# Attention and an ELU layer on one core: all of batch 0's q, k and v are issued ahead of the weights, and pairs 2 and 3 move into steps 0 to 3

## Chip, cores and metric

One core of one Trainium2 chip runs the kernel. The metric is device time in microseconds (us) of one execution, as the median of several runs. Differences within 0.3% count as no change here.

## What is computed

A sliding-window attention feeds a two-layer network with an ELU between the layers:

```python
# q, k, v: (8, 8, 576, 64) float32: batch, heads, positions, head size
scores = (q @ k.T) / sqrt(64)
scores = where(|pos_i - pos_j| <= 32, scores, -1e9)
attn = softmax(scores)               # over the keys
x = (attn @ v)                       # -> (8*576, 8*64) = (4608, 512)
h = x @ w_in                         # w_in (512, 2048)
g = where(h > 0, h, exp(min(h, 0)) - 1)
out = g @ w_out                      # w_out (2048, 512), out (4608, 512) float32
```

## The kernel before

The order of instructions on each engine is the order in which the program text issues them; nothing reorders them afterwards.

**Attention.** A batch has 9 blocks of 64 queries. Two blocks are a *pair*, and there are 36 pairs over the 8 batches; pairs 0 to 3 need batch 0 alone. `cast_qk` turns loaded float32 q and k (tile `f`, one for q and one for k) into bf16 (`qkb`), `transpose_qk` transposes these on TensorE into PSUM (`ptx`) and copies them to `qT` and `kT`. For a pair `scores` multiplies kT and qT into `psS` and takes the exponential into `pu` on ScalarE, `mask` multiplies by 0 or 1 into `pm` on VectorE, `pv` multiplies by v, `normalize` divides by the row sums into `x_st`, `x_transpose` transposes and `x_evac` copies the result into `xT`. Odd blocks read v shifted by 64 positions: `Vo` is a second copy of `Ve`, made by two DMAs on SP's queue in `rotate_v` (L122), each of which waits until the v loads that it reads have landed.

**Layer.** `xT[t]` holds 256 tokens (two pairs). The work on it is cut into 8 units of 256 hidden columns each, and the 18 tiles of 256 tokens give 144 steps. Step kk runs `mm1(kk)` (8 matmuls into `ps`, L435, then `e_sb` on ScalarE and `m_sb` on VectorE), and `mm2(kk - 2)` (4 matmuls into `psY`, L462); `elu` makes `g_sb` at the start of the step after. Steps 0 to 3 work on xT[0] (pairs 0 and 1), steps 4 to 7 on xT[1] (pairs 2 and 3), then the two alternate until step 15. Between these, attention tasks are put into named places of a step ("first", "dve", "mid", "end") by `at(step, place, ...)`, and they run in the loop

```python
run(kk, "first");  elu(kk - 1);  run(kk, "dve");  mm1(kk)
run(kk, "mid");    mm2(kk - 2);  run(kk, "end")
```

**Loads.** Queue q1 of the profile (hardware_dynamic) takes what SP issues: q and k, the `Vo` rotations, the outputs. Queue q0 (software_dynamic) takes what POOL issues: v and the weights, which are cast on the way. For batches 0 and 1, q and k come in halves of 288 positions, HALF_A and HALF_B. `gate(src)` (L130) is a DMA of one element on SP's queue that reads a piece of a weight tile; SP waits there until that weight's load has landed, and so holds back all that is behind it. w_in and w_out come in four chunks each; steps 0 and 1 need the first of w_in, steps 2 and 3 the second.

Of the kernel before, what the change touches and what calls it, by code (L numbers as in the profile page):

```python
# [15 lines left out]
def _bap(ap, new_ap, off=0):  # L16
    return bass.AP(tensor=ap.tensor, offset=ap.offset + off,
                   ap=[list(x) for x in new_ap])
# [3 lines left out]
def kernel(  # L22
# [15 lines left out]
    D_MODEL = H * D  # L38
# [8 lines left out]
    VS = 5  # L47
# [6 lines left out]
    NFO = D_FF // 128  # L54
# [39 lines left out]
    w_out_sb = wpool.tile([128, NFO, D_MODEL], BF16, name="w_out_sb")  # L94
# [4 lines left out]
    WHOLE, HALF_A, HALF_B = (0, SJ), (0, SJ // 2), (1, SJ // 2)  # L99
    qk_f = {}  # L100

    def load_qk(b, which, part):
        z, nj = part
        if (b, which) not in qk_f:
            qk_f[b, which] = lpool.tile([SP_, H * SJ * D], FP32,
                                        tag=f"f{which}", name=f"f{which}")
        t = qk_f[b, which]
        n = H * nj * D
        nc.sync.dma_start(
            out=t[:, z * n:(z + 1) * n].rearrange("p (h x) -> p h x", h=H),  # L110
            in_=(q, k)[which][b, :, z * SP_ * nj:(z + 1) * SP_ * nj, :]
            .rearrange("h (p j) d -> p h (j d)", j=nj))

    def load_v(b, m):
        lo = 128 * m - WIN
        p0 = max(0, -lo)
        p1 = min(128, S - lo)
        nc.gpsimd.dma_start(  # L118
            out=V_e[b % 3][p0:p1, m, :, 0:D],
            in_=v[b, :, lo + p0:lo + p1, :].rearrange("h p d -> p h d"))  # L120

    def rotate_v(b, m0=0, m1=VS - 1):  # L122
        e, o = V_e[b % 3], V_o[b % 3]
        nc.sync.dma_start(out=o[0:64, m0:m1], in_=e[64:128, m0:m1])
        nc.sync.dma_start(out=o[64:128, m0:m1], in_=e[0:64, m0 + 1:m1 + 1])
# [4 lines left out]
    def gate(src):  # L130
        n = gates[0]
        gates[0] += 1
        nc.sync.dma_start(out=gate_t[:, n:n + 1], in_=src)

    def load_w_in(c):
        w = D_FF // 4
        nc.gpsimd.dma_start(
            out=w_in_sb[:, :, c * w:(c + 1) * w],
            in_=moe_w_in[:, c * w:(c + 1) * w].rearrange(
                "(o p) f -> p o f", p=128))  # L140

    def load_w_out(c):
        n = NFO // 4
        nc.gpsimd.dma_start(
            out=w_out_sb[:, c * n:(c + 1) * n, :],
            in_=moe_w_out[c * n * 128:(c + 1) * n * 128, :].rearrange(
                "(o p) f -> p o f", p=128))

    def w_in_at(c):
        return w_in_sb[0:1, 0, (c + 1) * (D_FF // 4) - 1:(c + 1) * (D_FF // 4)]  # L150
# [9 lines left out]
    ident = cpool.tile([128, 128], BF16)  # L160
    make_identity(nc, ident)

    for which in range(2):
        load_qk(0, which, HALF_A)
    for m in (1, 2, 0):
        load_v(0, m)
    rotate_v(0, 0, 2)
    load_w_in(0)


# [16 lines left out]
        channel_multiplier=-1)  # L187
    kinds = ["FE", "EE", "EL", "LF"]

    for which in range(2):  # L190
        load_qk(0, which, HALF_B)
    for m in (3, 4):
        load_v(0, m)
    rotate_v(0, 2, VS - 1)
    load_w_out(0)
    load_w_in(1)
    load_w_out(1)
# [1 line left out]
    def kind(jb):  # L199
        qb = jb % NQB  # L200
        return "F" if qb == 0 else "L" if qb == NQB - 1 else "E"
# [10 lines left out]
    def cast_qk(b, which, part, hps, eng):  # L212
        z, nj = part
        hp0, nh = hps[0], 2 * len(hps)
        n = H * nj * D
        s_ = qk_f[b, which][:, z * n + 2 * hp0 * nj * D:
                            z * n + (2 * hp0 + nh) * nj * D]
        s_ = _bap(s_, [s_.ap[0], [nj * D, nh], [D, nj], [1, D]])
        t = lpool.tile([SP_, nj, nh * D], BF16, tag=f"b{which}", name="qkb",
                       bufs=4)  # L220
        qk_b[b, which, z, hp0] = t
        copy_on(eng, _bap(t, [t.ap[0], [D, nh], [nh * D, nj], [1, D]]), s_)

    def transpose_qk(b, which, part, hps, evac, tag="t0"):
        z, nj = part
        src = qk_b.pop((b, which, z, hps[0]))
        nh = len(hps)
        W = 512 if nh > 1 else 1024
        pt = ps_tile([128, nh, W], BF16, tag, "ptx")
        for g in range(nh):  # L230
            for j in range(nj):
                nc.tensor.transpose(  # L232
                    pt[:, g, j * SP_:(j + 1) * SP_],
                    src[:, j, g * 128:(g + 1) * 128], ident[0:SP_, 0:SP_])
        n = SP_ * nj
        if which == 0:
            T, c0 = qT[b % 2], z * n
        else:
            T, c0 = kT[b % 2], WIN + z * n
        d = T[:, hps[0]:hps[0] + nh, c0:c0 + n]  # L240
        pitch = d.ap[1][0] if nh > 1 else n
        copy_on(evac,
                _bap(d, [d.ap[0], [pitch, nh], [nj, SP_], [1, nj]]),
                _bap(pt, [pt.ap[0], [W, nh], [1, SP_], [SP_, nj]]))
# [3 lines left out]
    def scores(i, tag="s"):  # L248
        psS = ps_tile([128, 2, 512], FP32, tag, "psS")
        for z in range(2):  # L250
            jb = 2 * i + z
            b, qb = jb // NQB, jb % NQB
            for h in range(H):
                hp, base = h // 2, 64 * (h % 2)
                nc.tensor.matmul(  # L255
                    psS[:, h % 2, hp * 128 + z * QB:hp * 128 + (z + 1) * QB],
                    lhsT=kT[b % 2][base:base + 64, hp, QB * qb:QB * qb + 128],
                    rhs=qT[b % 2][base:base + 64, hp, QB * qb:QB * (qb + 1)],
                    start=True, stop=True)
        pu = apool.tile([128, H, 2 * QB], BF16, tag="pu")  # L260
        nc.scalar.activation(  # L261
            pu, _bap(psS, [psS.ap[0], [1, 1024]]), AX.Exp, scale=SCALE)
        st[i] = [psS, pu, None, None, tag]

    def mask(i):
        psS, pu, _, _, _ = st[i]
        pm = apool.tile([128, H, 2 * QB], BF16, tag="pm")
        m0 = kinds.index(kind(2 * i) + kind(2 * i + 1))
        mm = masks[:, m0:m0 + 2, :]
        nc.vector.tensor_mul(  # L270
            pm, pu, _bap(mm, [mm.ap[0], [0, H], [1, 2 * QB]]))
        st[i][2] = pm
# [50 lines left out]
    def front_qk(part, tags):  # L323
        for g in range(2):
            hps = (2 * g, 2 * g + 1)
            cast_qk(0, 0, part, hps, nc.vector)
            cast_qk(0, 1, part, hps, nc.scalar)
            transpose_qk(0, 0, part, hps, nc.scalar, tags[g])
            transpose_qk(0, 1, part, hps, nc.vector, tags[2 + g])

    front_qk(HALF_A, ("h0", "h1", "y0", "y1"))
    for i, tag in ((0, "s"), (1, "u")):
        scores(i, tag)
    for fn in (mask, pv, normalize, x_transpose, x_evac):
        for i in (0, 1):
            fn(i)

    gate(w_in_at(0))
    for which in range(2):
        load_qk(1, which, HALF_A)  # L340
    for m in range(3):
# [21 lines left out]
    def at(kk, slot, fn, *args):  # L363
        tasks.setdefault((kk, slot), []).append((fn, args))
# [11 lines left out]
        at(kk + 3, "dve", x_evac, i)  # L376


    at(1, "mid", front_qk, HALF_B, ("y0", "y1", "y0", "y1"))
    for i, tag in ((2, "s"), (3, "u")):  # L380
        at(1, "mid", scores, i, tag)
        at(2, "first", mask, i)
    for i in (2, 3):
        at(2, "first", pv, i)
        at(3, "dve", normalize, i)
        at(3, "mid", x_transpose, i)
        at(4, "dve", x_evac, i)
    at(4, "dve", swap_pools)

    allh = tuple(range(HP))  # L390
# [12 lines left out]
    for b in range(2, B):  # L403
        k0 = HALF * (first_pair(b) - 2)
        for n in range(2 * HP):
            if b == 2:
                which, hp, kk, ahead = n // HP, n % HP, 20 + n, 2
            else:
                which, hp, kk, ahead = n % 2, n // 2, k0 - 15 + 2 * n, 5
# [106 lines left out]
```

## Time and profile before

| | us |
|---|---|
| median of 3 runs (359.62 to 360.46) | 359.78 |
| the profiled execution's own time | 362.43 |
| its span, first to last instruction | 360.7 |
| TensorE (PE) busy | 319.6 |
| VectorE (DVE) busy | 254.3 |
| ScalarE (ACT) busy | 167.4 |

The profile is of one execution, which took 2.65 us more than the median of the runs. PE is busy for 89% of the span; in 40 slices of 9 us its busy share is below 8 tenths only in the first five (0, 3, 6, 2 and 7 tenths), the ninth (7) and the last (4). The granted TensorE clock is 0.969 of full speed over the span; it is about half in the fourth and fifth slices.

### The profile page before, as it was taken

What the parts mean: (1) busy time and instruction counts of PE and PEld (TensorE: products, weight loads), DVE (VectorE), ACT (ScalarE), POOL (GpSimd) and SP (SyncE); (2) the same over time, 40 slices, a digit from 0 to 9 for tenths busy, and PEclk for the clock granted to TensorE, in tenths of its full rate; (3) what the DMA queues carried; (4) which work ended last, traced back from release to release, by engine and by line L of the source; (5) the groups of instructions that cost most, each with busy time, mean ns of one, the idle gap of its engine ahead of it and who ended that gap; (6) DMA issues with size and microseconds to landing.
All of it is one profiled execution on the core that took longest, in us unless ns stands there. A gap on an engine that the chain in (4) does not pass through costs nothing.

```text
span 360.7 us, 8157 instructions
## 1 busy us (share of the span) xinstructions
PE 319.6 (89%) x3356; PEld 214.9 (60%) x3408; DVE 254.3 (71%) x474; ACT 167.4 (46%) x262; POOL 85.0 (24%) x108
## 2 busy tenths in 40 slices
PE   0362789979899999999999999999999999999994
PEld 0241556645666666666666666666666666666662
DVE  4442456858677877887877777878877777777763
ACT  2413227355565555355555544455545454434341
POOL 8711300452184400412520331421100000000000
PEclk9995599989999999999999999999999999999999
DMA  9999999779949966930778693963011210101011
GB/s 164 202 237 212 219 150 221 165 49 260 198 134 215 162 42 121 205 81 2 138 47 196 129 154 19 204 131 117 15 47 44 78 58 2 60 2 59 2 58 58
DMA packets 63944, 42.00 MB, mean 116 GB/s; under 512 B 38564, under 2 KB 58020, under 8 KB 63908
## 3 DMA queue, kind: packets, MB, share of 16 engines
q1 hardware_dynamic: 22180, 32.58, 37.8%
q0 software_dynamic: 41728, 8.92, 32.0%
q8 instruction: 26, 0.43, 0.5%
q14 instruction: 10, 0.08, 0.1%
HBM read 36.70 MB, written 9.44 MB: 128 GB/s over the span
## 4 chain that ended last, share of the span: by engine, by line
PE 73%; DVE 11%; DMA 7%; ACT 4%; issue 3%; SPq 0%; DVEq 0%
PE ps L435 33%; PE psY L462 29%; DMA f<-in_k_dram 7%; PE ptx L232 4%; DVE g_sb L448 3%; PE psS L255 3%; PE psS L282 3%; ACT e_sb L441 3%; PE psXT L303 2%; DVE m_sb L443 2%; DVE x_st L294 2%; DVE y_sb L471 1%; ACT qkb L208 1%; DVE pm L270 1%; DVE kT L210 1%
## 5 line engine op out<-in xcount | busy, mean ns | idle before, releaser
L441 ACT ACTIVATE e_sb<-ps 128x512 f32<-128x512 f32 x144 | 86.0, 597 | 167.6 <-PE ps L435 167.6
L435 PE MATMUL ps<-xT,w_in_sb 128*128 128x256 bf16 x1152 | 153.1, 277 | 5.6 <-DVE xT L313 4.7
L462 PE MATMUL psY<-w_out_sb,g_sb 128*128 128x512 bf16 x524 | 142.5, 382 | 3.2 <-issue 0.4
L435 PEld LDWEIGHTS <-w_in_sb 128*128 128x128 bf16 x1152 | 110.4, 99 | 37.8 <-issue 7.5
L443 DVE TENSOR_SCALAR m_sb<-e_sb 128x512 bf16<-128x512 f32 x144 | 71.0, 493 | 63.8 <-ACT e_sb L441 63.4
L448 DVE SCALAR_TENSOR_TENSOR g_sb<-ps,m_sb 128x512 bf16<-128x512 f32 x144 | 99.4, 690 | 13.6 <-PE psS L282 0.5
L462 PEld LDWEIGHTS <-g_sb 128*128 128x128 bf16 x576 | 51.1, 98 | 38.8 <-issue 1.1
L210 POOL CAST qkb<-f 96x768 bf16<-96x768 f32 x48 | 42.1, 900 | 120.5 <-PE ptx L232 51.8
L118 POOL DMA_DIRECT2D Ve<-in_v_dram x40 | 34.3, 862 | 51.6 <-PE psS L282 33.6
L232 PE MATMUL ptx<-ident,qkb 96*128 96x96 bf16 x384 | 28.2, 216 | 18.7 <-DVE qkb L210 11.0
L261 ACT ACTIVATE pu<-psS 128x1024 bf16<-128x1024 f32 x36 | 36.4, 1018 | 3.4 <-PE psS L255 3.3
L232 PEld LDWEIGHTS <-qkb 96*128 96x128 bf16 x384 | 23.9, 103 | 21.4 <-DVE qkb L210 11.7
L270 DVE TENSOR_TENSOR pm<-pu,masks 128x1024 bf16<-128x1024 bf16 x36 | 26.1, 726 | 3.8 <-ACT pu L261 3.6
L294 DVE TENSOR_TENSOR x_st<-psS,rc 128x512 bf16<-128x512 f32 x36 | 24.9, 692 | 1.2
L282 PEld LDWEIGHTS <-pm 128*64 128x64 bf16 x576 | 12.9, 115 | 18.9 <-DVE pm L270 9.1
L208 ACT COPY qT<-ptx 128x576 bf16<-128x576 bf16 (+1 forms) x30 | 20.0, 666 | 4.4 <-PE ptx L232 4.4
L282 PE MATMUL psS<-Ve,pm 128*64 128x65 bf16 x320 | 16.9, 202 | 3.2 <-DVE pm L270 3.2
L303 PEld LDWEIGHTS <-x_st 128*128 128x128 bf16 x144 | 9.6, 100 | 14.9 <-DVE x_st L294 12.9
L208 ACT COPY kT<-ptx 128x576 bf16<-128x576 bf16 (+1 forms) x26 | 17.4, 670 | 0.0
L255 PE MATMUL psS<-qT,kT 64*128 64x64 bf16 x576 | 15.5, 196 | 1.6 <-DVE kT L210 1.3
L303 PE MATMUL psXT<-ident,x_st 128*128 128x128 bf16 x144 | 14.6, 225 | 2.5 <-DVE x_st L294 2.1
L255 PEld LDWEIGHTS <-kT 64*128 64x128 bf16 x576 | 11.2, 98 | 8.9 <-issue 7.0
(29 smaller groups left out, 88.5 us busy)
## 6 DMA issues: line engine op xcount, KB each, us to landing
out_dram<-y_sb SPq DMA_DIRECT2D x18, 512.0 KB, 3.0
f<-in_q_dram SPq DMA_DIRECT2D x6, 1152.0 KB, 11.5
f<-in_k_dram SPq DMA_DIRECT2D x6, 1152.0 KB, 15.3
Vo<-Ve SPq DMA_DIRECT2D x12, 260.0 KB, 4.3
Ve<-in_v_dram POOLq DMA_DIRECT2D x24, 128.0 KB, 8.1
f<-in_q_dram SPq DMA_DIRECT2D x4, 576.0 KB, 12.3
f<-in_k_dram SPq DMA_DIRECT2D x4, 576.0 KB, 13.6
w_in_sb<-in_moe_w_in_dram POOLq DMA_DIRECT2D x4, 512.0 KB, 18.4
```

The source lines that it names most:

```text
L118: nc.gpsimd.dma_start(out=V_e[b % 3][p0:p1, m, :, 0:D], in_=v[b, :, lo + p0:lo + p1, :].rearrange("h p d -> p h d"))
L208: nc.scalar.copy(d_, s_)
L210: eng.tensor_copy(d_, s_)
L232: nc.tensor.transpose(pt[:, g, j * SP_:(j + 1) * SP_], src[:, j, g * 128:(g + 1) * 128], ident[0:SP_, 0:SP_])
L255: nc.tensor.matmul(psS[:, h % 2, hp * 128 + z * QB:hp * 128 + (z + 1) * QB], lhsT=kT[b % 2][base:base + 64, hp, QB * qb:QB * qb + 128], rh ...
L261: nc.scalar.activation(pu, _bap(psS, [psS.ap[0], [1, 1024]]), AX.Exp, scale=SCALE)
L282: nc.tensor.matmul(psS[QB * z:QB * (z + 1), par, hp * VD:(hp + 1) * VD], lhsT=pm[:, par * HP + hp, z * QB:(z + 1) * QB], rhs=vv[:, qb // 2 ...
L435: nc.tensor.matmul(ps[:, j, :], lhsT=w_in_sb[:, do, fo * 128:(fo + 1) * 128], rhs=xT[t][:, do, :], start=(do == 0), stop=(do == NDO - 1))
L441: nc.scalar.activation(e_sb, ps, AX.Exp)
L443: nc.vector.tensor_scalar(m_sb, e_sb, -1.0, None, ALU.add)
L448: nc.vector.scalar_tensor_tensor(g_sb, psH.pop(kk), 0.0, m_t.pop(kk), ALU.max, ALU.min)
L462: nc.tensor.matmul(psY[t][ts], lhsT=g_sb[:, j, ts * 128:(ts + 1) * 128], rhs=w_out_sb[:, s * FG + j, :], start=(s == 0 and j == 0), stop=( ...
```

## The change

The second half of batch 0's q and k is issued on SP's queue right behind the first, ahead of the first rotation, and all five v loads of batch 0 ahead of the first weight chunk on POOL's queue. Casting and transposing that half (`front_qk(HALF_B, ...)`) moves from the middle of step 1 to a place between the masks and the value products of pairs 0 and 1, with other PSUM tags. The tasks of pairs 2 and 3 start in step 0 where they started in step 1. The first gate now reads the last element that chunk 0 of w_out brings, where it read w_in's chunk 0. No instruction is added or removed.

```diff
--- before.py
+++ after.py
@@ -160,11 +160,13 @@
     ident = cpool.tile([128, 128], BF16)
     make_identity(nc, ident)
 
-    for which in range(2):
-        load_qk(0, which, HALF_A)
-    for m in (1, 2, 0):
+    for part in (HALF_A, HALF_B):
+        for which in range(2):
+            load_qk(0, which, part)
+    for m in (1, 2, 0, 3, 4):
         load_v(0, m)
     rotate_v(0, 0, 2)
+    rotate_v(0, 2, VS - 1)
     load_w_in(0)
 
 
@@ -187,11 +189,6 @@
         channel_multiplier=-1)
     kinds = ["FE", "EE", "EL", "LF"]
 
-    for which in range(2):
-        load_qk(0, which, HALF_B)
-    for m in (3, 4):
-        load_v(0, m)
-    rotate_v(0, 2, VS - 1)
     load_w_out(0)
     load_w_in(1)
     load_w_out(1)
@@ -331,11 +328,14 @@
     front_qk(HALF_A, ("h0", "h1", "y0", "y1"))
     for i, tag in ((0, "s"), (1, "u")):
         scores(i, tag)
-    for fn in (mask, pv, normalize, x_transpose, x_evac):
+    for i in (0, 1):
+        mask(i)
+    front_qk(HALF_B, ("h0", "h1", "y0", "y1"))
+    for fn in (pv, normalize, x_transpose, x_evac):
         for i in (0, 1):
             fn(i)
 
-    gate(w_in_at(0))
+    gate(w_out_sb[0:1, NFO // 4 - 1, D_MODEL - 1:D_MODEL])
     for which in range(2):
         load_qk(1, which, HALF_A)
     for m in range(3):
@@ -376,15 +376,13 @@
         at(kk + 3, "dve", x_evac, i)
 
 
-    at(1, "mid", front_qk, HALF_B, ("y0", "y1", "y0", "y1"))
     for i, tag in ((2, "s"), (3, "u")):
-        at(1, "mid", scores, i, tag)
-        at(2, "first", mask, i)
-    for i in (2, 3):
-        at(2, "first", pv, i)
-        at(3, "dve", normalize, i)
-        at(3, "mid", x_transpose, i)
-        at(4, "dve", x_evac, i)
+        at(0, "mid", scores, i, tag)
+        at(1, "dve", mask, i)
+        at(1, "mid", pv, i)
+        at(2, "dve", normalize, i)
+        at(2, "mid", x_transpose, i)
+        at(3, "dve", x_evac, i)
     at(4, "dve", swap_pools)
 
     allh = tuple(range(HP))
```

SP's queue, from the start of the program: before, where f_115 and f_117 are q and k of batch 0, and f_280 q of batch 1:

```order
L109 DMA f_115<-in_q_dram 96x8x192
L109 DMA f_117<-in_k_dram 96x8x192
L124 DMA Vo_91<-Ve_88 64x1040
L125 DMA Vo_91<-Ve_88 64x1040
L109 DMA f_115<-in_q_dram 96x8x192
L109 DMA f_117<-in_k_dram 96x8x192
L124 DMA Vo_91<-Ve_88 64x1040
L125 DMA Vo_91<-Ve_88 64x1040
L133 DMA gate_t<-w_in_sb 1x1
L109 DMA f_280<-in_q_dram 96x8x192
```

and now, where f_320 is q of batch 1:

```order
L109 DMA f_115<-in_q_dram 96x8x192
L109 DMA f_117<-in_k_dram 96x8x192
L109 DMA f_115<-in_q_dram 96x8x192
L109 DMA f_117<-in_k_dram 96x8x192
L124 DMA Vo_91<-Ve_88 64x1040
L125 DMA Vo_91<-Ve_88 64x1040
L124 DMA Vo_91<-Ve_88 64x1040
L125 DMA Vo_91<-Ve_88 64x1040
L133 DMA gate_t<-w_out_sb 1x1
L109 DMA f_320<-in_q_dram 96x8x192
```

Both loads of the second half have moved ahead of the four rotation DMAs, and the gate reads w_out.

VectorE, from the evacuation of xT of pairs 0 and 1 to the masks of pairs 2 and 3, before:

```order
L313 COPY xT<-psXT 128x4x128 x2
L443 TENSOR_SCALAR m_sb<-e_sb 128x512
L448 SCALAR_TENSOR_TENSOR g_sb<-ps,m_sb 128x512
L443 TENSOR_SCALAR m_sb<-e_sb 128x512
L210 CAST qkb<-f_115 96x4x3x64
L210 COPY kT_86<-ptx 128x2x288
L210 CAST qkb<-f_115 96x4x3x64
L210 COPY kT_86<-ptx 128x2x288
L270 TENSOR_TENSOR pm<-pu,masks 128x1024 x2
```

and now, from behind the masks of pairs 0 and 1 to the masks of pairs 2 and 3:

```order
L207 CAST qkb<-f_115 96x4x3x64
L207 COPY kT_86<-ptx 128x2x288
L207 CAST qkb<-f_115 96x4x3x64
L207 COPY kT_86<-ptx 128x2x288
L288 RECIPROCAL rc<-psS 128x8
L291 TENSOR_TENSOR x_st<-psS,rc 128x512
L288 RECIPROCAL rc<-psS 128x8
L291 TENSOR_TENSOR x_st<-psS,rc 128x512
L310 COPY xT<-psXT 128x4x128 x2
L441 TENSOR_SCALAR m_sb<-e_sb 128x512
L446 SCALAR_TENSOR_TENSOR g_sb<-ps,m_sb 128x512
L267 TENSOR_TENSOR pm<-pu,masks 128x1024 x2
```

The two casts and two copies of the second half have moved from behind steps 0 and 1's `m_sb` to ahead of the first reciprocal, and the masks of pairs 2 and 3 follow the first `g_sb`.

## Rows read from the trace of the kernel before

**Rows 1.** The chain that ended last, in time order: start us, length us, what.

```profile
13.10 16.71 DMA f<-in_k_dram
...
39.34 0.65 PE psS L282 x16
...
43.52 1.69 PE ps L435 x8
...
47.80 1.03 PE ps L435 x8
...
49.70 0.87 PE ps L435 x8
...
75.37 1.53 PE ps L435 x8
...
79.43 0.89 PE ps L435 x8
```

**Rows 2.** Busy time by stretch (us): each engine, granted clock, DMA share, GB/s.

```profile
28.00:45.00 17.00, 9.18 (x101) 6.41 (x103) 6.31 (x12) 5.27 (x7) 4.44 (x6) 0.50 1.34 216
45.00:72.00 27.00, 25.04 (x244) 16.82 (x246) 18.56 (x34) 12.55 (x18) 4.77 (x6) 1.00 1.55 180
...
76.00:79.00 3.00, 3.00 (x21) 1.94 (x19) 0.43 (x1) 1.70 (x3) 1.01 (x2) 0.50 0.13 5
```

**Rows 3.** The timeline, 1 to 73 us: start, length, engine, line [idle before <-releaser].

```profile
1.50 2.66 POOL L118 DMA_DIRECT2D Ve<-in_v_dram  x3
...
8.59 0.83 ACT L208 CAST qkb<-f 96x768 bf16<-96x768 f32 x1 [2.39 <-DMA f<-in_k_dram]
...
12.93 0.76 DVE L210 COPY kT<-ptx 128x576 bf16<-128x576 bf16 x1 [1.23 <-PE ptx L232]
...
15.42 1.53 DVE L270 TENSOR_TENSOR pm<-pu,masks 128x1024 bf16<-128x1024 bf16 x2 [1.73 <-ACT pu L261]
...
17.96 0.95 PEld L282 LDWEIGHTS <-pm 128*64 128x64 bf16 x31 [1.67 <-DMA Vo<-Ve]
...
21.60 3.33 PE L435 MATMUL ps<-xT,w_in_sb 128*128 128x256 bf16 x16 [0.52 <-DVE xT L313]
...
36.08 0.93 PE L255 MATMUL psS<-qT,kT 64*128 64x64 bf16 x28 [0.63 <-DVE kT L210]
...
54.58 1.46 ACT L208 CAST qkb<-f 96x1536 bf16<-96x1536 f32 x1
...
72.45 1.46 ACT L208 CAST qkb<-f 96x1536 bf16<-96x1536 f32 x1
```

**Rows 4.** DMA queues, 2:6 us, then 25:33 us: packets, MB, share.

```profile
q1 hardware_dynamic: 1223, 0.93, 100.5%
...
q1 hardware_dynamic: 1852, 1.54, 90.0%
q0 software_dynamic: 1847, 0.27, 46.6%
```

**Rows 5.** SP's queue on the timeline: start us, us to issue, line, DMA.

```profile
11.25 0.54 SPq L124 DMA_DIRECT2D Vo<-Ve  x1
...
19.85 4.79 SPq L109 DMA_DIRECT2D f<-in_k_dram  x1
...
46.75 0.55 SPq L109 DMA_DIRECT2D f<-in_k_dram  x1
```

**Rows 6.** The rotation issued at 11.84 us (tile Vo): time to landing.

```profile
DMA to landing us min/median/max: 6.1/6.1/6.1
```

**Rows 7.** The rotation issued at 15.02 us (tile Vo): time to landing.

```profile
DMA to landing us min/median/max: 15.2/15.2/15.2
```

**Rows 8.** w_in's first chunk, issued at 4.14 us (tile w_in_sb): time to landing.

```profile
DMA to landing us min/median/max: 8.9/8.9/8.9
```

**Rows 9.** Loads of batch 1, half A (tile f): landing, k the longest.

```profile
DMA to landing us min/median/max: 14.2/15.7/17.2
```

**Rows 10.** Loads of batch 1, half B (tile f): landing, k the longest.

```profile
DMA to landing us min/median/max: 10.3/11.9/13.6
```

## Prediction

> **What bounds the kernel now.** I read the chain that ended last first, then the timeline of the first 80 us, then the DMA queues. After about 80 us the chain is step work on PE, and the change leaves every instruction there as it was. So only the start matters, and its worth is how much earlier step 4 begins. Step 4 is the first that needs xT of pairs 2 and 3; from it on both kernels have the same order on every engine.
>
> The chain shows one wait that stands out: k's second half is issued at 13.10 us and takes 16.71 us to land, at 29.81 [rows 1]. Behind it come cast, transposes, scores, masks and values of pairs 2 and 3, and mm1 of step 4 starts at 47.80. Steps 0 and 1 had long been computed (21.60 to 24.93 [rows 3]). The wait also costs clock: from 28 to 45 us PE is busy for 9.18 of 17 us at a granted 0.50, the lower of its two levels (1.2 of 2.4 GHz), and from 45 us it has 1.00 [rows 2]. The reader sees the level in the matmuls: 8 of mm1 take 1.69 us from 43.52, and 0.87 from 49.70 [rows 1]. The 16 of steps 0 and 1 took 3.33 us [rows 3], 0.21 each, as at the low level, although the view lists no lower clock there; so I take that the kernel starts at the low level.
>
> **The change, term by term.** I follow the new order up to mm1(4).
>
> *When the second half is there.* From 2 to 6 us only q1 moves, at 0.93 MB in 4 us, or 0.23 MB per us [rows 4]. Two more loads of 0.59 MB take 5.1 us at that rate. The first k landed by 8.59 us, where ACT casts it [rows 3], so the second lands at about 13.7; if v's packets take every second turn, later, at about 15.5. Either is early: DVE's masks of pairs 0 and 1 end at 15.42 + 1.53 = 16.95 [rows 3], and DVE must cast q behind them. The 13 us wait is gone.
>
> *front_qk of the second half.* The first half took from 8.59 to 13.69 [rows 3], and its last transposes ended before the copy at 12.93, so about 4.4 us after the start. From 16.95 that is 21.4 for the earliest start of pv.
>
> *The rotations.* In the kernel before, pv waited for Vo and went on at 17.96 [rows 3]. Vo's first DMA is issued when v has landed, at 11.25 [rows 5]. v is on q0, and q0 moved nothing from 2 to 6 us, though POOL issued its first loads from 1.50 on [rows 3]: they moved when q1 had run dry. With 5.1 us more on q1 it starts 5.1 us later, so Vo is issued at 16.35, its second DMA 0.6 later at 16.95, and this takes 6.1 us to land [rows 6]: 23.05. From pv to mm1 took 21.60 - 17.96 = 3.64 us [rows 3]. So mm1(0) starts at 26.7 if Vo decides, at 25.0 if front_qk does. I take 26.5, near the upper. That is 4.9 later than before: this part is a loss, hidden only by the larger gain behind it.
>
> One rule bears on this term. The queues do alternate when both run: 1852 and 1847 packets in 8 us [rows 4]. The Trainium skill (DMA: Bandwidth & Descriptors, Queues, rings and completion order) says that an engine goes round robin between the rows that have work, packet by packet; the rows from 25 to 33 us agree with it, the silence of q0 before 6 us does not. By that rule v would share from the start, the 2816 rows of the first three v loads (two of 128 x 8, one of 96 x 8) would be through at 231 per us by 14.3 us, Vo would land by about 21.0, front_qk would decide, and the sum would end 1.5 us lower, at 350.1. The sum goes by the rows.
>
> *Steps 0 to 3.* PE now does, at the low level: four mm1 (4 x 1.69 = 6.8), two mm2 with as many columns each as a mm1 (3.4), scores of two pairs (32 matmuls, 28 took 0.93 [rows 3]: 1.1), pv of two pairs (2 x 0.65 [rows 1] = 1.3), 8 transposes of half a mm1 matmul each (0.85): 13.4. Waits for masks and x_st I put at 0.5, an estimate: a mask takes 0.7 us [rows 3] and lies beside mm1(1), normalizing beside mm1(2), almost wholly. Sum 14.0. If the clock rose 5 us after mm1(0), the 9 us left would halve, but masks and x_st would then be late: I put this end at 11.5. If it rises only in step 5, step 4 takes up to 0.8 more: 14.8. Before, it rose at 45 [rows 2], 5 us into unbroken step work; here unbroken work begins with mm2(0), 9 us after mm1(0), so the rise falls about on step 4. I take 13.9. Step 4 then starts at 26.5 + 13.9 = 40.4, against 47.80: 7.4 us gained.
>
> *Later stalls.* Before, the clock fell once more (0.50 from 76 to 79 [rows 2]); mm1(16) to mm1(17), 75.37 to 79.43, took 4.06 us [rows 1], about half of it owed to the clock. The steps now meet POOL's casts and the transfers, which are held by DMA, at other places, so this fall may stay away, or the steps lose a little elsewhere. I bound it by -0.7 (a mask, the largest piece that DVE could be late with) and +1.8, and take +0.8 as about the middle.
>
> *Hidden.* POOL issues two v loads more ahead of making the masks (three took 2.66 us [rows 3], so 1.8): between nothing and 1.8 us, and I take nothing, since DVE waited for pu alone at 15.42 [rows 3]. w_in's first chunk landed 8.9 us after 4.14, at 13.0 [rows 8]; 5.1 us more, and two v loads of 1792 rows ahead of it, at most 7.8 us at 231 rows per us, make 25.9, before 26.5. The gate on w_out's first chunk moves batch 1's loads: k's half A was issued at 19.85 and took 17.2 us [rows 5, 9]; 5.1 us later it lands at 42. Its cast stood 6.8 us behind mm1(4) (54.58 [rows 3]), now at 47.2: 5 us of cover. Half B of k landed at 46.75 + 13.6 = 60.35 [rows 5, 10], held by DMA volume that does not change; its cast at 72.45 [rows 3] comes to 65.0: 4.7 us of cover. Beyond the cover each us late costs a us.
>
> Sum: 7.4 + 0.8 = 8.2 us. The profiled execution took 362.43 and would take 354.2 (span 352.5); the median is 2.65 lower: 359.78 - 8.2 = **351.6**.
>
> **Rivals.**
>
> *Transfers become the bound.* Batch 1's k half A lands after 47.2, or half B after 65.0. For it: DMA is busy throughout these stretches (share above 1 [rows 2]), and the gate now stands behind a later load. Against: q1 has no second half of batch 0 ahead of that load any more. Half A at 50.8 gives back 3.6 us: 355.2; at 55.4 everything.
>
> *The clock rises early.* If the scores and mm1 of steps 0 and 1 suffice, step 4 starts 2.4 us sooner: 349.2. With front_qk deciding, not Vo, 347.7. Against: from 39.34 to 45 it took all of pv and 5 us of steps.
>
> *Slower: Vo stuck behind the second half.* The rotation that was issued right behind these loads before took 15.2 us to land [rows 7]. If the new first rotation does the same from 16.95, Vo lands at 32.2, mm1(0) starts at 35.8, step 4 at 49.7: 1.9 later, 361.7. It decides from a landing at 30.3 on, 13.3 us after issue. Against: by 16.35 the loads ahead are through, by 13.7 or 15.5. The Trainium skill (DMA: Bandwidth & Descriptors, Queues, rings and completion order) has each engine consume a queue's descriptors in ring order, and so speaks against this change: Vo now stands behind two loads more. The 15.2 agrees with it.
>
> *The change does not do what it says.* k's second half still lands near 30, since q0 takes turns. Then nothing moves: 359.8.
>
> **How the numbers follow.** Forecast 0.62 (own range 349.3 to 354.3: mm1(0) between 25.0 and 27.5, steps 0 to 3 between 13 and 14.8, later stalls from -0.7 to +1.8, not all at one end together), clock early 0.14, transfers 0.14, unchanged 0.03, slower 0.07. The range 347.7 to 355.8 leaves out the worse half of the transfers' case, the last two and a little of the rest. 0.3% (1.1 us) is about what a measurement can tell from no change: faster 0.89, same 0.04 (the unchanged case and a bit of the transfers'), slower 0.07.
>
> **What would show it.** In the new profile: ACT's second cast of k near 16.3, with no wait for DMA; pv waiting for Vo and going on near 23; mm1(0) near 26.5; no empty stretch on PE from 27 to 40; mm1(4) near 40.4, with the clock at 1.00 from about there; the two casts of batch 1's half A and B without a DMA wait. The prediction fails if a v load or the rotations land 5 us later than worked out here, if the casts near 47 and 65 wait for DMA, or if the clock stays low beyond step 5.

## The result, and the profile after

The kernel with the change takes 352.04 us (median of 4 runs, 351.06 to 352.33) against 359.76 for the kernel before on the same chip (4 runs, 359.62 to 360.46). The ratio is 0.9777, with a 95% interval of 0.9754 to 0.98: 7.7 us faster.

The profiled execution took 352.11 us by its own time. Its page gives the span, the busy times with their share, and PE's busy tenths in 40 slices of 8.8 us:

```profile
span 350.4 us, 8157 instructions
...
PE 314.8 (90%) x3356; PEld 212.4 (61%) x3408; DVE 256.2 (73%) x474; ACT 167.2 (48%) x262; POOL 84.2 (24%) x108
...
PE   0347999688999999999999999999999999999994
```

The hole of before in the fourth and fifth slices is gone; PE is full from the fifth slice on, with a dent in the eighth to tenth (6, 8 and 8 tenths). PE is busy for 4.8 us less than in the profile of before, with as many instructions: fewer of them ran at the lower clock.

The chain that ended last shows the start (columns as in [rows 1]):

```profile
16.60 6.18 DMA Vo<-Ve
22.82 0.66 PE psS L279 x15
...
26.47 1.86 PE ps L433 x8
...
32.02 0.69 DVE g_sb L446
32.86 0.69 DVE x_st L291
33.70 0.70 DVE x_st L291
...
37.44 0.87 PE ps L433 x8
```

The 16.71 us of k [rows 1] no longer stand in it. The rotation `Vo` takes their place, with 6.18 us. mm1(0) starts at 26.47, where before it was 21.60 [rows 3], and mm1(4) at 37.44, where before it was 47.80 [rows 1]. The timeline of the same execution (columns as in [rows 3]) tells who waited:

```profile
1.50 4.31 POOL L118 DMA_DIRECT2D Ve<-in_v_dram  x5
...
15.67 0.83 ACT L205 CAST qkb<-f 96x768 bf16<-96x768 f32 x1
...
20.66 0.13 PEld L279 LDWEIGHTS <-pm 128*64 128x64 bf16 x1
22.82 0.95 PEld L279 LDWEIGHTS <-pm 128*64 128x64 bf16 x31 [2.03 <-DMA Vo<-Ve]
...
29.23 1.31 PE L433 MATMUL ps<-xT,w_in_sb 128*128 128x256 bf16 x8
...
32.01 1.05 PE L433 MATMUL ps<-xT,w_in_sb 128*128 128x256 bf16 x8
```

ACT casts k's second half at 15.67 without a wait. PE has the transposes behind it at 20.66 and stands 2.03 us for `Vo`. The three mm1 of 26.47, 29.23 and 32.01 take 1.86, 1.31 and 1.05 us for the same 8 matmuls: they get faster within the second, near 30 us, as at a rise from the lower to the higher of the two levels (1.2 and 2.4 GHz).

The DMA queues from 7 to 8 us, from 9 to 12 us and from 13 to 14 us (columns as in [rows 4]):

```profile
q1 hardware_dynamic: 301, 0.22, 109.0%
q0 software_dynamic: 61, 0.01, 11.9%
...
q1 hardware_dynamic: 767, 0.58, 92.8%
q0 software_dynamic: 762, 0.10, 49.6%
...
q0 software_dynamic: 1080, 0.14, 213.7%
q1 hardware_dynamic: 46, 0.03, 14.4%
```

POOL issued v from 1.50 on, but q0 moved its first packets only between 7 and 8 us; from 9 us on the two queues took turns, until q1 ran out between 13 and 14 us. The Trainium skill (DMA: Bandwidth & Descriptors, Queues, rings and completion order) has an engine go round between the rows that have work: the rows from 9 to 12 us agree, 762 packets to 767. Up to 7 us q0 moved nothing, and no run here shows whether its row had work by then.

### The profile page after: what moved, and what is told of

Same layout as the page of the kernel before. It is cut to its first block, busy times and chain, and to the rows that moved or that the text cites. A ratio compares the mean times of both kernels' runs of the same rounds, so it can differ in the third digit from the quotient of the medians.

```text
span 350.4 us, 8157 instructions
## 1 busy us (share of the span) xinstructions
PE 314.8 (90%) x3356; PEld 212.4 (61%) x3408; DVE 256.2 (73%) x474; ACT 167.2 (48%) x262; POOL 84.2 (24%) x108
## 4 chain that ended last, share of the span: by engine, by line
PE 73%; DVE 14%; ACT 4%; DMA 4%; issue 3%; SPq 0%; DVEq 0%
PE ps L433 32%; PE psY L460 28%; PE ptx L229 4%; DVE g_sb L446 4%; PE psS L252 3%; DVE x_st L291 3%; PE psXT L300 3%; PE psS L279 3%; ACT e_sb L439 3%; DVE m_sb L441 2%; DMA f<-in_k_dram 2%; DVE y_sb L469 2%; DMA Vo<-Ve 2%; DVE pm L267 2%; ACT pu L258 1%
## 5 line engine op out<-in xcount | busy, mean ns | idle before, releaser
L433 PE MATMUL ps<-xT,w_in_sb 128*128 128x256 bf16 x1152 | 150.7, 274 | 4.2 <-DVE xT L310 3.3
L460 PE MATMUL psY<-w_out_sb,g_sb 128*128 128x512 bf16 x524 | 141.0, 379 | 3.0 <-DVE g_sb L446 0.2
L433 PEld LDWEIGHTS <-w_in_sb 128*128 128x128 bf16 x1152 | 109.1, 98 | 34.7 <-issue 4.8
L441 DVE TENSOR_SCALAR m_sb<-e_sb 128x512 bf16<-128x512 f32 x144 | 72.0, 500 | 59.9 <-ACT e_sb L439 59.5
L267 DVE TENSOR_TENSOR pm<-pu,masks 128x1024 bf16<-128x1024 bf16 x36 | 27.8, 773 | 2.3 <-ACT pu L258 2.1
L279 PE MATMUL psS<-Vo,pm 128*64 128x65 bf16 x256 | 14.5, 201 | 2.7 <-DMA Vo<-Ve 1.9
```

Source lines behind the costliest of these rows:

```text
L267: nc.vector.tensor_mul(pm, pu, _bap(mm, [mm.ap[0], [0, H], [1, 2 * QB]]))
L279: nc.tensor.matmul(psS[QB * z:QB * (z + 1), par, hp * VD:(hp + 1) * VD], lhsT=pm[:, par * HP + hp, z * QB:(z + 1) * QB], rhs=vv[:, qb // 2 ...
L433: nc.tensor.matmul(ps[:, j, :], lhsT=w_in_sb[:, do, fo * 128:(fo + 1) * 128], rhs=xT[t][:, do, :], start=(do == 0), stop=(do == NDO - 1))
L441: nc.vector.tensor_scalar(m_sb, e_sb, -1.0, None, ALU.add)
L460: nc.tensor.matmul(psY[t][ts], lhsT=g_sb[:, j, ts * 128:(ts + 1) * 128], rhs=w_out_sb[:, s * FG + j, :], start=(s == 0 and j == 0), stop=( ...
```

## The experiments

The label of an execution stands for its profile, and e_sb(n) for the start of step n's exponential on ACT, which marks the step. Three groups shared a chip and the runs of the kernel before: the first four kernels here (before: 360.48, 19 runs), the next four (360.01, 11), the last two (360.34, 11).

**before_again: the kernel before, unchanged, once more.**

> The kernel before, unchanged, profiled once more. The profile of before took 362.43 us beside a median of 359.76, and the profile of the changed kernel 352.11 beside 352.04, so the two profiles differ by 10.3 us and the medians by 7.7. If the 2.65 us belong to that one execution (its clock fell again from 76 to 79 us), this profile is near 359.8 and shows step 4 near 47.8 and no second fall of the clock. If the profile of before always takes longer than its runs (a cost of profiling), it is near 362.4 again, and the changed kernel hides the cost in some way.

Its own time was 359.7 us, 2.7 less than the profile that the prediction was made from. Its chain, and its windows from 28 to 45 and 76 to 79 us (columns as in [rows 2]):

```profile
13.52 15.79 DMA f<-in_k_dram
...
46.72 1.03 PE ps L435 x8
```

```profile
28.00:45.00 17.00, 9.21 (x108) 6.17 (x108) 6.82 (x13) 5.87 (x8) 4.20 (x5) 0.60 1.33 217
...
76.00:79.00 3.00, 2.75 (x27) 1.78 (x25) 3.00 (x4) 2.87 (x5) 3.00 (x5) 1.00 0.31 20
```

The wait for k is nearly the same (15.79 us for 16.71), but mm1(4) starts 1.08 us earlier and the clock does not fall from 76 to 79 us as it did in [rows 2]. One of the two profiled executions has that second fall and the other has not, so it is not fixed in the kernel; the changes are compared with this profile from here on.

**loads_only: the new loads and gate, the old places of the second half and of pairs 2 and 3.**

```diff
-    for i in (0, 1):
-        mask(i)
-    front_qk(HALF_B, ("h0", "h1", "y0", "y1"))
-    for fn in (pv, normalize, x_transpose, x_evac):
+    for fn in (mask, pv, normalize, x_transpose, x_evac):
...
+    at(1, "mid", front_qk, HALF_B, ("y0", "y1", "y0", "y1"))
...
-        at(0, "mid", scores, i, tag)
+        at(1, "mid", scores, i, tag)
```

(and each later task of pairs 2 and 3 back where it was)

> The new order of loads and the new gate, with the second half still transposed in step 1 and pairs 2 and 3 as before. By the sum of the prediction this alone gains nothing: mm1(0) waits for the rotation until about 26.5, the second half is cast behind step 1 at about 31, and from there to step 4 it took 18 us before (29.84 to 47.80), so step 4 comes at 47.5 to 49: 359 to 361 us. By the rival that the 13 us wait for k was simply the loss, and that taking it away is the gain, it is as fast as the changed kernel: 352 to 354.

Measured: 362.11 us (360.46 to 363.74, 10 runs), ratio 1.0051 (1.0023 to 1.0078). Its chain:

```profile
17.02 5.51 DMA Vo<-Ve
...
26.21 3.51 PE ps L432 x16
...
49.35 1.03 PE ps L432 x8
```

The second half is there early, but it is not used early: behind mm1 at 26.21 the chain still goes through its casts, transposes, scores and masks, and PE runs dry among them. `Vo` lands at 22.53, and pv starts then, where in [rows 3] it went on at 17.96. Step 4 is 2.6 us later than in before_again. Having k early is worth nothing alone; by the medians it costs 1.6 us.

**order_only: the old loads and gate, the new order.**

```diff
-    for part in (HALF_A, HALF_B):
-        for which in range(2):
-            load_qk(0, which, part)
-    for m in (1, 2, 0, 3, 4):
+    for which in range(2):
+        load_qk(0, which, HALF_A)
+    for m in (1, 2, 0):
...
-    rotate_v(0, 2, VS - 1)
```

(the second half's loads and rotation go back behind the masks' making, the gate back to w_in)

> The new order of casts, transposes and pairs, with the loads and the gate as before. k's second half lands near 29.8 and now holds back pairs 0 and 1 too: pv near 34.2, mm1(0) near 37.9, and 11 us (as in the changed kernel) to step 4 at 48.9: 361 us, up to 364 if the clock rises late. By the rival that the compact order of steps 0 to 3 and the clock that it keeps up are the gain, whatever the loads do, it is 354 to 357.

Measured: 360.06 us (358.93 to 362.34, 10 runs), ratio 0.9999 (0.9972 to 1.0026). Its chain:

```profile
12.82 14.99 DMA f<-in_k_dram
...
35.80 1.87 PE ps L436 x8
...
47.07 0.87 PE ps L436 x8
```

Now pairs 0 and 1 stand behind the late k too, so mm1(0) waits until 35.80. Steps 0 to 3 then take 11.27 us, as in the kernel after (10.97), and step 4 comes out where it was. No gain alone either.

**late_pairs: the kernel after, with the tasks of pairs 2 and 3 one step later, as before.**

```diff
-        at(0, "mid", scores, i, tag)
-        at(1, "dve", mask, i)
-        at(1, "mid", pv, i)
+        at(1, "mid", scores, i, tag)
+        at(2, "first", mask, i)
+    for i in (2, 3):
+        at(2, "first", pv, i)
```

(and normalize, x_transpose and x_evac to steps 3, 3 and 4)

> The changed kernel, with the tasks of pairs 2 and 3 one step later, where they stood before. mm1(0) stays at 26.5. Followed through VectorE (masks ahead of elu(1), normalizing behind elu(2), copies to xT behind elu(3)) step 4 starts near 40.5 instead of 37.4: 355 us (354 to 357). By the rival that DMA or the start of mm1(0) decides alone, and the place of pairs 2 and 3 does not matter, 352.

Measured: 354.29 us (353.48 to 354.74, 4 runs), ratio 0.9831 (0.9784 to 0.9877). Its chain:

```profile
26.30 3.47 PE ps L434 x16
...
33.65 1.83 PE ps L434 x8
...
40.88 1.03 PE ps L434 x8
```

mm1(0) starts as in the kernel after, but between the scores and the values of pairs 2 and 3 PE waits for exponentials and masks until 33.00, mm1(2) still runs at the lower clock (1.83 where after has 1.05), and step 4 is 3.4 us later than after's. From loads_only step 4 comes 8.5 us earlier by putting the second half ahead of step 0 (49.35 to 40.88), and 3.4 more by starting pairs 2 and 3 in step 0.

**after_again: the kernel after, unchanged, for the three below.**

> The changed kernel once more, as a yardstick beside the three others of this call. 352.0 us (351.1 to 352.4) and a ratio near 0.978. By the theory that VectorE beside POOL costs it something after step 17, VectorE's masks and m_sb between 68 and 78 us are again longer (up to 1.7 and 1.0 us) than elsewhere (0.69 and 0.43).

Measured: 351.48 us (350.14 to 352.35, 6 runs), ratio 0.9744 (0.9715 to 0.9773).

**gate_back: the first gate reads w_in's first chunk again.**

```diff
-    gate(w_out_sb[0:1, NFO // 4 - 1, D_MODEL - 1:D_MODEL])
+    gate(w_in_at(0))
```

> The changed kernel with the gate on w_in's first chunk, as before. Batch 1's half A is then issued some 4 us sooner and competes with the second chunks of the weights. By the sum this costs and brings nothing, since half A has about 7 us of cover in the changed kernel: 352.0, within 0.3%. By the rival that the new gate is a part of the gain (weights in time for steps 2 and 3), w_in's second chunk lands up to 4 us later, about when mm1(2) wants it (32.0), and step 4 is 1 to 3 us late: 353 to 355.

Measured: 350.98 us (350.16 to 353.04, 6 runs), ratio 0.9741 (0.9712 to 0.977): the same as after_again. That part of the change does nothing to the time that can be measured. The execution that was profiled took 353.04, the longest of the six, and VectorE's timeline shows where:

```profile
71.77 2.25 DVE L441 TENSOR_SCALAR m_sb<-e_sb 128x512 bf16<-128x512 f32 x1 [1.21 <-ACT e_sb L439]
```

One `m_sb` takes 2.25 us, beside POOL's casts and v issues of batch 2 (67.10 to 77.6); in after_again the same one takes 0.43. e_sb(18) is 0.05 us behind after_again's, e_sb(24) 2.64 behind.

**vo_direct: the first rotation of batch 0 is replaced by two loads from v itself, on POOL's queue, so that nothing waits for v to land first.** The column of ones is set once.

```diff
+    nc.vector.memset(V_o[0][:, 0:2, :, D:VD], 1.0)
...
-    for m in (1, 2, 0, 3, 4):
+    for m in (1, 2, 0):
+        load_v(0, m)
+    for m in range(2):
+        nc.gpsimd.dma_start(
+            out=V_o[0][:, m, :, 0:D],
+            in_=v[0, :, 128 * m + WIN:128 * (m + 1) + WIN, :]
+            .rearrange("h p d -> p h d"))
+    for m in (3, 4):
         load_v(0, m)
-    rotate_v(0, 0, 2)
```

> The changed kernel, with the part of Vo that pairs 0 and 1 read loaded straight from v (two more v loads on POOL's queue) in place of the first rotation. If the rotation's landing decides mm1(0), as the prediction has it, pv starts when the second half's transposes are through (20.7) in place of 22.8, mm1(0) near 24.4 and everything behind it 2.1 us earlier: 349.9. If something else decides (the transposes, or DMA volume, which grows by 2048 rows), 352 or later.

Measured: 352.03 us (350.14 to 353.11, 6 runs), ratio 0.9764 (0.9734 to 0.9795). e_sb(0) starts at 26.62, 1.9 us ahead of after_again's 28.53, and e_sb(15) is still 1.6 ahead (59.99 to 61.62). Then VectorE's cast of batch 1's half B on the timeline, and below it the chain:

```profile
61.48 0.96 DVE L214 CAST qkb<-f 96x1536 bf16<-96x1536 f32 x1 [0.43 <-DMA f<-in_k_dram]
```

```profile
47.70 13.76 DMA f<-in_k_dram
...
63.42 1.62 PE ps L440 x8
...
67.48 0.89 PE ps L440 x8
```

The wait for the rotation did set the start, as the prediction said. But half B's k lands at 61.46, not earlier than in after (60.7); the cast waits, PE pauses, and mm1(16) runs at the lower clock: 1.62 us. mm1(17) starts 0.5 us later than after_again's. All that was won at the start is lost at step 16.

**b2_act: batch 2's eight casts on ScalarE, where POOL did them.**

```diff
-            at(kk - ahead, "mid", cast_qk, b, which, WHOLE, (hp,), nc.gpsimd)
+            at(kk - ahead, "mid", cast_qk, b, which, WHOLE, (hp,),
+               nc.scalar if b == 2 else nc.gpsimd)
```

> The changed kernel, with the eight casts of batch 2 on ScalarE in place of POOL. The changed kernel is 9.7 us ahead of the second profile of before at step 18 and 8.0 at step 22; POOL's casts and v issues lie beside VectorE there, whose mask takes 1.68 us in place of 0.69. If POOL's casts cost that, this gives back 0.5 to 1.8 us: 350.2 to 351.5. If the v issues or the transfers cost it, 352; if ScalarE's 0.83 us casts are late for e_sb, 353 or more.

Measured: 349.98 us (349.53 to 350.85, 5 runs), ratio 0.9709 (0.9683 to 0.9735), by the medians 1.5 us less than after_again; the two profiled executions are 0.57 apart (350.85 and 351.42), and the intervals of the two ratios overlap a little. VectorE's groups from 66 to 82 us, by line, in after_again and then in b2_act (busy, mean ns | idle before):

```profile
L441 DVE TENSOR_SCALAR m_sb<-e_sb 128x512 bf16<-128x512 f32 x7 | 4.6, 659 | 3.8 <-ACT e_sb L439 3.7
...
L267 DVE TENSOR_TENSOR pm<-pu,masks 128x1024 bf16<-128x1024 bf16 x2 | 2.3, 1141 | 0.2 <-ACT pu L258 0.2
```

```profile
L442 DVE TENSOR_SCALAR m_sb<-e_sb 128x512 bf16<-128x512 f32 x7 | 3.0, 427 | 5.2 <-ACT e_sb L440 5.2
L267 DVE TENSOR_TENSOR pm<-pu,masks 128x1024 bf16<-128x1024 bf16 x2 | 1.4, 682 | 0.0
```

The same operations take 6.9 us beside POOL's work and 4.4 without it. Up to e_sb(19) the two kernels run alike (73.29 to 73.27); e_sb(22) is 0.76 ahead, e_sb(30) 1.06, the last one 0.58. The edit takes two things away, though: without the casts ahead of them POOL's v issues of batch 2 move from about 70 us to 50.77, so the run does not tell casts from issues.

**vo_gate: vo_direct, and the second gate waits for the third chunk of w_in where it waited for the fourth.** Half B is then issued at 43.45, where in vo_direct it was 47.70.

```diff
-    gate(w_in_at(3))
+    gate(w_in_at(2))
```

> The changed kernel with Vo's first part loaded straight from v, as in the run before, and the second gate on w_in's third chunk in place of its fourth, so that batch 1's half B is issued some 5 us sooner. By the theory that Vo sets mm1(0) and that half B's late landing (61.46, when VectorE wanted to cast it at 61.05) took the 1.9 us back, half B now lands by 58, step 16 keeps its lead and the time is 349.6 (351.5 less 1.9). By the rival that the start is not worth anything because the whole flow of transfers sets the pace, or because w_in's fourth chunk now is late for step 12, it stays at 351.5 or more.

Measured: 349.66 us (349.06 to 351.06, 5 runs), ratio 0.9709 (0.9682 to 0.9736). The time came as expected, the way did not: the lead of 1.8 us at e_sb(0) is 1.5 at e_sb(6) and 0.22 at e_sb(12). Half A's k, issued at 27.95, takes 17.34 us, and the cast waits for it until 45.3, where vo_direct had it at 43.1. The cause of that long transfer is open, and the next run, with the same loads, does not have it (12.8 us). What is left is won behind step 18. VectorE's groups from 66 to 82 us:

```profile
L448 DVE TENSOR_SCALAR m_sb<-e_sb 128x512 bf16<-128x512 f32 x7 | 3.6, 513 | 4.6 <-ACT e_sb L446 4.6
L274 DVE TENSOR_TENSOR pm<-pu,masks 128x1024 bf16<-128x1024 bf16 x2 | 1.4, 710 | 0.0
```

POOL's casts begin at 72.00 in it, 4 us later than in after (67.88), and the masks fall beside less of them. 5.0 us where after_again had 6.9 goes with the gain; no run here moved POOL's work alone, so this is read, not shown.

**best: vo_gate and b2_act together.**

> The same, with batch 2's casts on ScalarE too. If the two costs are separate (the start, 1.9 us; VectorE beside POOL's casts, 1.5 us, as measured), the time is 348.1. If the casts on ScalarE now wait for batch 2's load, whose landing near 68 does not move while the steps come 1.9 us sooner, 349 to 350.

Measured: 349.98 us (349.13 to 351.98, 6 runs), ratio 0.9711 (0.968 to 0.9741). The lead over after_again stays at 2.0 us to e_sb(12) and 1.8 to e_sb(18); then comes a cast of batch 2:

```profile
72.90 0.83 ACT L212 CAST qkb<-f 96x768 bf16<-96x768 f32 x1 [2.09 <-DMA f<-in_q_dram]
```

e_sb(19) starts at 73.64, 0.4 later than in after_again. Two gains of about 1.8 and 1.5 us do not add: ScalarE's wait for batch 2's q takes 2.2 us of the lead back at step 19. The medians of the three last kernels lie 1.5 to 1.8 us below after_again's, on two chips, and they cannot be told from each other.

## Why the prediction was right

The time was foretold as 351.6 and came as 352.04. The mechanism held: from step 4 on the kernel is what it was, so the start of step 4 decides most of it. Own time less the start of mm1(4) is 314.67 us in after, 312.98 in before_again, 314.39 in loads_only, 314.04 in order_only and 313.13 in late_pairs, while that start goes from 37.44 to 49.35. But two terms and the base were mis-sized, and the errors nearly cancel: that the sum came within 0.44 us is partly luck.

**When the second half is there.** Right: ACT's cast at 15.67 without a wait (16.3 foretold), the transposes through at 20.66 (21.4). Loads_only and order_only add what the prediction did not say: the early k and the new order are worth nothing one by one, and 7.7 us together.

**The rotations.** Right within 0.4 us in its times: `Vo` issued at 16.02 and 16.60 (16.35 and 16.95), landed after 6.18 us (6.1), pv on at 22.82 (23.05), mm1(0) at 26.47 (26.5). The reason given for them, that v "moved when q1 had run dry", holds only in part. Before, q0's first packets came between 6 and 7 us, as q1 ran out; here they came between 7 and 8 us, and q1 had work until after 13. So q0 shared for 5 us, at about 250 packets per us beside q1 and 1080 once q1 was nearly through: that sharing brought `Vo`'s issue only 0.3 us ahead of the forecast. That `Vo` and not the transposes decides is shown by vo_direct, where e_sb(0) comes 1.9 us earlier.

**Steps 0 to 3.** Mis-sized: 13.9 us foretold, 10.97 measured. The step that failed is "unbroken work begins with mm2(0), 9 us after mm1(0), so the rise falls about on step 4". PE's work was unbroken from mm1(0) to about 30.5 us, as the row from 28 to 30 us shows (columns as in [rows 2]):

```profile
28.00:30.00 2.00, 2.00 (x39) 1.46 (x38) 0.89 (x2) 1.63 (x3) 0.00 (x0) 1.00 1.71 195
```

By the length of mm1(1) the clock rose about 3.5 us after mm1(0), in step 1 (an estimate from 1.31, 1.86 and 0.87 us). So the sum ended below the 11.5 that the prediction gave for an early rise, the waits for masks and `x_st` included that it saw coming. This was the rival "the clock rises early" (step 4 at 40.4 - 2.4 = 38.0), in the start of step 4 though not in the time.

**Later stalls.** Mis-sized: +0.8 foretold, bounds -0.7 to +1.8. Against the profile that the term was worked out from it came as 0.0: the lead grew from 10.53 us at step 15 to 12.68 at step 17, where that profile's clock falls, and was 10.32 at the end. Against before_again, which has no such fall, it came as -1.7: step 4 is 9.28 us earlier, the end only 7.6. Where the 1.7 go is seen in ACT's e_sb(18) and e_sb(24), in before_again and then in after:

```profile
80.64 0.60 ACT L441 ACTIVATE e_sb<-ps 128x512 f32<-128x512 f32 x1 [1.12 <-PE ps L435]
...
95.62 0.60 ACT L441 ACTIVATE e_sb<-ps 128x512 f32<-128x512 f32 x1 [2.18 <-PE ps L435]
```

```profile
70.90 0.60 ACT L439 ACTIVATE e_sb<-ps 128x512 f32<-128x512 f32 x1 [1.12 <-PE ps L433]
...
87.65 0.60 ACT L439 ACTIVATE e_sb<-ps 128x512 f32<-128x512 f32 x1 [2.18 <-PE ps L433]
```

The lead is still 9.74 us at step 18 and 7.97 at step 24; at step 36 it is 7.58, and nothing changes it from there on. The size varies with the execution: from step 18 to the end after_again's lead falls by 1.3 us, from 9.55 to 8.28. What lies at steps 18 to 22 in after is POOL's batch 2 and a slow VectorE:

```profile
67.88 2.56 POOL L207 CAST qkb<-f 96x768 bf16<-96x768 f32 x3 [21.04 <-DMA f<-in_q_dram]
...
73.00 1.68 DVE L267 TENSOR_TENSOR pm<-pu,masks 128x1024 bf16<-128x1024 bf16 x1
...
74.59 1.04 DVE L441 TENSOR_SCALAR m_sb<-e_sb 128x512 bf16<-128x512 f32 x1
```

A mask takes 1.68 us here and 0.69 at 58.42 in the same execution. POOL starts when q of batch 2 lands, at about the same time in both kernels (67.32 in before_again), and the steps have moved under it by 9 us. b2_act shows that this neighbour costs the kernel after something, 1.5 us by the medians and 0.57 by the profiled executions. The bound of -0.7, "a mask, the largest piece that DVE could be late with", was the error: one `m_sb` in gate_back was 1.8 late. How much of it the kernel before pays as well stays open: its `m_sb` from 60 to 84 us are slow too (684 ns each in before_again), and it was not run with the casts on ScalarE. So that this neighbour makes the whole -1.7 is argued, not shown.

**The base.** "The median is 2.65 lower" was taken to hold for the new kernel too, and did not: before's profile was an execution with a fall of the clock that before_again lacks, while after's, at 352.11, is at its median. From profile to profile the gain is 10.3 us, from median to median 7.7. In the prediction's own terms, against the profile it used: step 4 came 10.36 us earlier (7.4 foretold), the later stalls 0.0 (+0.8), and the 2.65 of the base were 0.07 for the new kernel. The errors of +3.0, -0.8 and -2.6 leave -0.4. Against before_again the terms read 9.28 and -1.7: errors of 1.9 and -2.5, which leave 7.6 for the 8.2.

**Covers.** Both casts of batch 1 went without a wait for DMA, as foretold. The prediction took ScalarE's casts of batch 1 (54.58 and 72.45 [rows 3]) for k's, but these are of q; k's are on VectorE, about 0.5 us later. Half A's k landed at 36.8 ahead of its cast at 44.55, 7.7 us of cover (5 foretold). Half B's landed at 60.7 ahead of 62.41, 1.7 us (4.7 foretold): step 4 came earlier and the load 0.4 later. vo_direct used up this cover, and lost all it had won. So the rival "transfers become the bound" did not happen here, but in vo_direct it did. Neither of "Vo stuck" (6.18 us, not the 15.2 of [rows 7]) and "does not do what it says" happened.

## What to carry to other kernels

Making data early and using it early are one change: the first alone delays what now waits behind it, the second alone ties more work to the late transfer, and only both take the wait off the path. Count for each later load how long before its use it lands, since moving the start up by more than the smallest of these covers gains nothing further. Take two profiles of the kernel before costing anything to the last us: a single one may hold a fall of the clock that is not the kernel's.

## What the runs showed of the hardware

VectorE's `m_sb` and masks, which here read no PSUM, grew beside POOL's casts and v issues: `m_sb` from 0.43 us to between 0.69 and 1.04 and once to 2.25, a mask from 0.69 to as much as 1.68. `g_sb` and `x_st`, which read PSUM, kept their 0.69 in the same stretch.

The clock did not rise at the same point of the same steps, not even in executions of one kernel. mm1(1) starts 2.8 us after mm1(0) and took 1.31 us in after, 1.17 in after_again and 1.89 in order_only, vo_direct and b2_act; mm1(2), 5.5 to 5.8 us after mm1(0), took 1.05 in all of these.

And the windows of after list a granted clock of 1.00 from 20 to 28 us, in which mm1(0) takes 1.86 us for what later takes 0.87: near the start the length of the matmuls tells the level better than that column does.
